# First key weights in three loads, first x turned in four parts, and a new written order for one gated attention kernel

## The chip, the cores and the metric

The kernel runs on one core of one Trainium2 chip. A time is the device time of one execution in microseconds (us). Before the change three runs gave 263.52, 263.54 and 266.09 us, with a median of 263.54 us. The engines are named as in the profile: PE is the matrix engine (PEld is its weight load), DVE, ACT and POOL are the vector, scalar and general engines, and SP only issues DMAs.

## What is computed

The input is x (2048 rows, 512 columns, bf16). Two branches are computed from it and mixed, row by row, by a gate:

```
g = sigmoid(sum(x * gate_w))                 one number per row
q, k, v = x @ wq, x @ wk, x @ wv             32 heads of 16, cut into 4 segments of 512 rows
for each segment s:
    a_dot = softmax(q k^T / 4 + causal mask) v             inside the segment
    a_mem = phi(q) M / (phi(q) z + 1e-6)                   memory of the segments before
    o     = sigmoid(beta) * a_mem + (1 - sigmoid(beta)) * a_dot
    M, z  = M + phi(k)^T v, z + sum(phi(k))                phi(t) = t+1 if t>0 else exp(t)
a = concat(o) @ wo
b = (gelu(x @ w_gate) * (x @ w_up)) @ w_down               inner width 1792
out = g * a + (1 - g) * b
```

`beta` has one value per head.

## The kernel before

**Tiling.** The work is cut into four segments (the first digit in a name: `K2_3` belongs to segment 2). A segment has x transposed in SBUF (`xT`, 512 by 512), and these groups of work, each of which holds one PSUM bank while PE fills it and until another engine has emptied it:

- `K`, `Q` (four groups each, four matmuls of 512 columns), `V` (eight half groups of four matmuls of 256 columns), `G` and `U` (14 each, the gate and up projections) and their evictions `Kev`, `Qev`, `Vev`, `Gev`, `gd` (gelu while evicting) and `h` (multiply by the up projection);
- the scores: 18 fills `st` a segment, which write all four banks of `psX`, one exponential `exp` on ACT for each (128 by 2048), and the causal mask on POOL (`msk`). `kpada` and `kpadb` on DVE spread k for the fills;
- `pv` (scores times v), whose result is turned and normalised on DVE (`tp`, `pvp`, `ota`), the memory read (`nd`, `ndp`, `otr`, `otm`) and write (`ktr`, `mz`, `mza`, `mzq`), and the outputs (`out` with `wev`, `wo` with `oev`, and the store `dma`).

There are four single PSUM banks for all groups other than `st`; the digit behind a colon in the order is the bank (`G0_5:3`), a letter is the engine of an eviction (`:a` ACT, `:d` DVE).

**What sets the order.** The order of all work is written out by hand in the string `ORDER` (some thousand words). The program walks through it, appends each task's instructions to the queue of its engine, and puts a semaphore wait before an instruction where data or a buffer is not free. Each engine then takes its own queue strictly in that order; an instruction that waits holds up all behind it on its engine. The waits on semaphores of DMAs are the same kind of wait. SP's DMA issues are a queue like the others.

**The start.** Two row blocks of the first x (`x0_0`, `x0_1`) are loaded and turned by PE against an identity matrix (`xtr0`, L786), the result is copied from `psX` to `xT` (`xev0`, L795); the other two row blocks come by transposing DMAs (`x0_t2`, `x0_t3`, L361). Until x has arrived PE multiplies constants (`warm1`, `warm2`, L383; 45 and 7 matmuls of 80 columns). The first K (L477) is computed in three kinds of pieces: `a` (input blocks 2 and 3, the first 256 rows), `b` (blocks 0 and 1, the same rows) and `c` (all four blocks, the last 256 rows, for which `x0_t2` and `x0_t3` must have landed). wk is loaded in two halves: blocks 2, 3 from SP and 0, 1 from ACT (L341).

**Other lines that matter here.** `ld_xt` (L345) loads x of a later segment in four transposing DMAs; those of segment 1 wait for `wv` to have landed. `ld_beta` loads beta to 128 partitions (8 KB in all), `betab` (L764, DVE, four copies) sorts it by head and waits for that load; `bexp` and `gqa`, `gqb`, `gfull` make the mixing factors from it. `vsh` (L518) moves 64 partitions of `vnat` by DMA as soon as the `Vev` of its four half groups are done. An order of loads within SP can hold a wait that is in the load's own list (`["wo"]`, `["wu0"]`) only if that other load stands earlier in `ORDER`.

Of the kernel before, what the change touches and what calls it, by code (L numbers as in the profile page):

```python
# [248 lines left out]
def _build(es, nc, A_x, A_wq, A_wk, A_wv, A_wo, A_beta, B_w_gate, B_w_up, B_w_down, gate_w, out):  # L249
# [132 lines left out]
    for name, n, cols in (("warm1", 45, 80), ("warm2", 7, 80)):  # L382
        one(name, PE, 3.0, [I(lambda e, cols=cols: e.matmul(BK[s0.i][:, 0:cols], ones, ones[:, 0:cols], start=True, stop=True),  # L383
                              [], [bk(s0)]) for _ in range(n)], bias=9000.0, opens=name == "warm1")
# [400 lines left out]
    for p in (1, 0):  # L785
        one(f"xtr0_{p}", PE, 4 * T_TR, [I(lambda e, q=q, kb=kb, p=p: e.transpose(  # L786
            XB[:, 1024 * p + (kb % 2) * 256 + q * 128:1024 * p + (kb % 2) * 256 + q * 128 + 128],
            pt[stage[0]][:, q, kb * 128:(kb + 1) * 128], ident[:, :]),
            [("xs", 0, 0), ("xs", 0, 1), ("pt", stage[0]), ("ident",)], [("X", p)]) for kb in (2 * p, 2 * p + 1) for q in (0, 1)])
        dst = xT[0][:, 2 * p:2 * p + 2, 0:256]  # L790
        xin = XB[:, 1024 * p:1024 * p + 512].rearrange("p (k c) -> p k c", c=256)
        wr = [("xT", 0, kb, "h0") for kb in (2 * p, 2 * p + 1)]
        task(f"xev0_{p}", [
            (ACT, 0.477, [I(lambda e, dst=dst, xin=xin: e.activation(dst, xin, ACTF.Copy), [("X", p)], wr)]),
            (DVE, 0.335, [I(lambda e, dst=dst, xin=xin: e.tensor_copy(dst, xin), [("X", p)], wr)])], L_DVE)  # L795
# [79 lines left out]
U0_13:3 U0_10:2 h0_10 Q2_1:1 Qev2_1:d exp0_2C st0_2D mz0:0 U0_7:2 U0_9:1 pvp0_10 h0_13 exp0_2D phqb1_0 st0_2E exp0_2E phka1_0 h0_7 mza0 h0_9 ota0_0
phqa1_2 kpadb1_0 G1_4:3 U0_1:2 h0_1 Gev1_4:a V1_1b:0 st0_3A G1_0:1 U0_5:3 Q2_2:2 exp0_3A Vev1_1b:a Gev1_0:a Qev2_2:a kpadb1_1 st0_3B exp0_3B U0_11:0
U0_4:1 U0_12:2 st0_3C phkb1_0 exp0_3C phqc1_0 kpada1_2 h0_4 h0_5 U0_6:1 U0_2:3 h0_11 h0_12 phqb1_2 h0_2 G1_3:0 Gev1_3:d h0_6 kpadb1_2 st0_3D phka1_2
U0_3:2 h0_3 U0_8:3 h0_8 Q2_3:0 Qev2_3:d exp0_3D phkb1_2 msk0_2A msk0_2B msk0_2C msk0_3A msk0_2E msk0_2D msk0_3C goc0 msk0_3B st1_0A msk0_3D pv0_3:1230
exp1_0A st1_0B exp1_0B tp0_d20 tp0_d21 pvp0_20 tp0_d30 ota0_1 pvp0_21 tp0_d31 kpada1_3 out0_1_0:1 out0_1_1 out0_1_2 V2_0a:2 Vev2_0a:d G1_9:3 V2_1b:0
Vev2_1b:d wev0_1:d st1_0C G1_8:2 G1_10:0 G1_11:1 gelu1 gd1_9 G1_7:3 gd1_8 gd1_10 gd1_7 gd1_11 G1_13:2 gd1_13 G1_12:0 gd1_12 phqc1_2 phkc1_0 mzq0  # L880
pvp0_31 pvp0_30 ota0_3 V2_0b:3 Vev2_0b:d ota0_2 V2_1a:1 Vev2_1a:d out0_0_0:2 out0_0_1 out0_0_2 nd1_0:0 ndp1_0 phkc1_2 exp1_0C st1_0D exp1_0D K2_0:3
K2_2:1 wev0_0:d Kev2_0:d Kev2_2:a K2_1:0 st1_0E Kev2_1:d U1_2:2 h1_2 wo0_1:1 nd1_3:3 nd1_1:0 exp1_0E st1_1A ld_x3_2 vsh1_00 vsh2_01 ktr1_1 ktr1_0
oev0_1 ndp1_1 wo0_0:2 oev0_0 kpada2_0 vsh1_21 out0_2_0:1 nd1_2:0 msk1_0C msk1_0A exp1_1A st1_1B exp1_1B msk1_0B gz1 msk1_0E msk1_1A msk1_0D msk1_1B
out0_2_1 wo0_2:2 ndp1_2 st1_1C exp1_1C nd1_5:0 out0_2_2 ndp1_3 wev0_2:a ndp1_5 out0_3_0:3 st1_1D nd1_4:0 out0_3_1 out0_3_2 ktr1_2 dma0 vsh1_01 otr1_3
ndp1_4 otr1_0 oev0_2 phka2_0 msk1_1C wev0_3:d ktr1_3 dma1 vsh2_00 otr1_1 ld_x3_1 ld_x3_0 ld_x3_3 exp1_1D st1_2A exp1_2A gr1 msk1_1D pv1_1:1023 st1_2B
exp1_2B tp1_d01 tp1_d00 kpadb1_3 V2_2b:0 Vev2_2b:d K2_3:1 Kev2_3:a G2_3:0 pvp1_00 Gev2_3:d tp1_d10 st1_2C U1_8:1 G2_1:0 otr1_2 V2_3a:2 h1_8 Gev2_1:d
Vev2_3a:d kpadb2_0 kpadb2_1 exp1_2C st1_2D phkb2_0 exp1_2D G2_6:1 wo0_3:0 U1_3:2 pvp1_01 tp1_d11 Gev2_6:a h1_3 phka2_2 oev0_3 st1_2E U1_0:3 V2_3b:1
G2_0:2 Gev2_0:d h1_0 Vev2_3b:d exp1_2E phkb2_2 st1_3A mz1:0 G2_4:2 G2_5:3 pvp1_10 mza1 Gev2_5:d exp1_3A st1_3B exp1_3B Gev2_4:d U1_11:1 G2_2:0
Gev2_2:d ota1_0 U1_13:3 h1_13 U1_10:2 h1_10 h1_11 G2_11:0 G2_10:3 pvp1_11 phkc2_0 phkc2_2 ota1_1 otm1_0 otm1_1 G2_12:2 G2_9:1 st1_3C gelu2 gd2_11
gd2_12 G2_7:0 G2_13:2 gd2_10 gd2_9 gd2_7 gd2_13 G2_8:3 gd2_8 U1_7:1 U2_9:0 K3_0:2 h1_7 U2_5:3 Q3_0:1 phqa2_0 h2_9 h2_5 Qev3_0:d Kev3_0:d exp1_3C  # L890
st1_3D exp1_3D U1_1:0 U2_12:3 msk1_3A msk1_2A msk1_3B U2_13:1 h2_12 h1_1 h2_13 kpada2_1 st2_0A U1_9:2 V2_2a:3 U2_7:0 msk1_2D msk1_2B msk1_2E h1_9
Vev2_2a:d vsh2_20 dma2 dma3 ktr2_0 ktr2_2 vsh2_21 exp2_0A phqb2_0 msk1_3D msk1_2C msk1_3C st2_0B h2_7 kpada2_2 pv1_3:1230 tp1_d21 exp2_0B tp1_d20
V3_1a:2 Vev3_1a:a st2_0C exp2_0C pvp1_21 tp1_d31 U1_6:1 Q3_1:2 V3_0a:0 st2_0D h1_6 pvp1_20 Vev3_0a:d Qev3_1:a V3_2b:1 U1_4:2 U1_5:0 exp2_0D st2_0E
exp2_0E tp1_d30 phqc2_0 h1_5 h1_4 ota1_2 Vev3_2b:a U1_12:3 h1_12 pvp1_31 pvp1_30 out1_1_0:0 st2_1A V3_1b:2 out1_1_1 V3_3a:3 exp2_1A st2_1B msk2_0B
msk2_0D Vev3_3a:a exp2_1B out1_1_2 U2_4:1 msk2_0E goa1 gob1 kpadb2_3 kpada2_3 msk2_0C msk2_0A msk2_1A ota1_3 h2_4 otm1_2 otm1_3 K3_1:3 mzq1 Vev3_1b:a
wev1_1:a st2_1C msk2_1B goc1 U2_1:2 Q3_3:1 V3_0b:0 Kev3_1:d kpada3_0 h2_1 Qev3_3:d kpadb2_2 exp2_1C msk2_1C st2_1D V3_2a:3 U2_6:2 exp2_1D Vev3_2a:a
wo1_1:1 Vev3_0b:d kpadb3_0 h2_6 oev1_1 st2_2A msk2_1D pv2_1:0231 exp2_2A st2_2B exp2_2B tp2_d00 pvp2_00 phqa2_2 tp2_d01 tp2_d10 pvp2_10 pvp2_01
tp2_d11 out1_0_0:0 out1_0_1 st2_2C phqb2_2 out1_0_2 V3_3b:2 Vev3_3b:d wev1_0:d out1_3_0:3 phqc2_2 pvp2_11 exp2_2C st2_2D exp2_2D wo1_0:1 out1_3_1
# [46 lines left out]
```

## Time and profile before

| What | Value |
|---|---|
| Median of three runs | 263.54 us |
| The profiled execution's own time | 263.46 us |
| Its span, first to last instruction | 261.7 us |
| Around the span (263.46 - 261.7) | 1.8 us |
| PE busy | 257.5 us, 98% of the span |
| ACT, DVE, POOL busy | 203.2, 198.0 and 98.4 us |
| 72 exponentials (L609) | 1877 ns each |
| Moved by DMA | 16.50 MB |

The span runs from the first to the last instruction of the core. The busy time of PE contains modelled ends of matmuls, so that a busy PE is not yet PE at its peak pace; the chain of waits and the times at which matmuls begin tell more. A row of the timeline is: start, duration, engine, line, operation, out<-in, count, and in brackets the idle time before it and what ended that. For a DMA the duration is that of its issue; the list of DMA issues gives the time from the start of an issue to the last byte's landing.

### The profile page before, as it was taken

What the parts mean: (1) busy time and instruction counts of PE and PEld (TensorE: products, weight loads), DVE (VectorE), ACT (ScalarE), POOL (GpSimd) and SP (SyncE); (2) the same over time, 40 slices, a digit from 0 to 9 for tenths busy, and PEclk for the clock granted to TensorE, in tenths of its full rate; (3) what the DMA queues carried; (4) which work ended last, traced back from release to release, by engine and by line L of the source; (5) the groups of instructions that cost most, each with busy time, mean ns of one, the idle gap of its engine ahead of it and who ended that gap; (6) DMA issues with size and microseconds to landing.
All of it is one profiled execution on the core that took longest, in us unless ns stands there. A gap on an engine that the chain in (4) does not pass through costs nothing.

```text
span 261.7 us, 6706 instructions
## 1 busy us (share of the span) xinstructions
PE 257.5 (98%) x2849; PEld 122.1 (47%) x2849; DVE 198.0 (76%) x412; ACT 203.2 (78%) x171; POOL 98.4 (38%) x163
## 2 busy tenths in 40 slices
...
DMA packets 31990, 16.50 MB, mean 63 GB/s; under 512 B 21592, under 2 KB 31960, under 8 KB 31960
## 3 DMA queue, kind: packets, MB, share of 16 engines
...
q10 hardware_dynamic: 688, 0.85, 1.0%
...
q14 instruction: 8, 0.07, 0.1%
...
## 4 chain that ended last, share of the span: by engine, by line
PE 98%; DVE 0%; issue 0%; DVEq 0%
PE psD L449 48%; PE psD L735 19%; PE psX L602 9%; PE psD L644 6%; PE psD L499 6%; PE psD L749 5%; PE psD L477 1%; PE psD L547 1%; PE psD L383 1%; PE psD L577 1%; DVE xT L795 0%; DVE ost L753 0%; PE psX L786 0%; DVEq L818 0%; PE psD L769 0%
## 5 line engine op out<-in xcount | busy, mean ns | idle before, releaser
L609 ACT ACTIVATE pt<-psX 128x2048 bf16<-128x2048 f32 x72 | 135.1, 1877 | 28.3 <-PE psX L602 26.8
L615 POOL TENSOR_TENSOR pt<-pt,ctri 128x256 bf16<-128x256 bf16 x128 | 91.8, 727 | 129.2 <-ACT pt L609 124.7
L449 PE MATMUL psD<-xT,wu 128*128 128x512 bf16 x224 | 54.6, 380 | 0.0
L449 PE MATMUL psD<-xT,wg 128*128 128x512 bf16 x224 | 53.4, 379 | 0.0
L735 PE MATMUL psD<-wd,gb 128*128 128x512 bf16 x224 | 53.2, 380 | 0.0
L720 DVE TENSOR_TENSOR gb<-psD,gb 128x512 bf16<-128x512 f32 x56 | 37.2, 681 | 10.8 <-PE psD L449 10.7
L449 PEld LDWEIGHTS psD<-xT,wg 128*128 128x128 bf16 x224 | 20.8, 98 | 24.7 <-issue 1.3
L735 PEld LDWEIGHTS psD<-wd,gb 128*128 128x128 bf16 x224 | 20.7, 98 | 24.3 <-issue 2.1
L449 PEld LDWEIGHTS psD<-xT,wu 128*128 128x128 bf16 x224 | 20.2, 98 | 24.7 <-issue 2.6
L602 PE MATMUL psX<-qT,kD 32*128 32x192 bf16 (+7 forms) x512 | 28.6, 287 | 0.0
L530 DVE STREAM_TRANSPOSE tT<-psD 128x512 f32<-128x512 f32 x32 | 21.8, 701 | 5.4 <-PE psD L644 4.9
L443 DVE CAST gb<-psD 128x512 bf16<-128x512 f32 x20 | 13.6, 688 | 13.0 <-PE psD L449 13.0
L602 PEld LDWEIGHTS psX<-qT,kD 32*128 32x128 bf16 x512 | 8.2, 92 | 25.1 <-ACT pt L609 13.6
L499 PE MATMUL psD<-wv,xT 128*128 128x257 bf16 (+1 forms) x128 | 18.2, 273 | 0.0
L753 DVE SCALAR_TENSOR_TENSOR ost<-psD,gtok,wds 128x512 bf16<-128x512 f32 (+1 forms) x17 | 11.9, 711 | 7.7 <-PE psD L749 7.6
L668 DVE SCALAR_TENSOR_TENSOR ob<-tT,gq,rc 128x256 bf16<-128x256 f32 x32 | 16.7, 522 | 1.1
L703 ACT ACTIVATE gb<-psD 128x512 bf16<-128x512 f32 x28 | 15.0, 594 | 3.3 <-PE psD L449 3.2
L644 PE MATMUL psD<-pt,vsh 64*17 64x192 bf16 (+7 forms) x512 | 17.1, 283 | 0.0
L644 PE MATMUL psD<-pt,vnat 64*17 64x192 bf16 (+7 forms) x512 | 17.1, 283 | 0.0
L449 PE MATMUL psD<-xT,wq 128*128 128x512 bf16 x64 | 16.3, 379 | 0.0
L749 PE MATMUL psD<-wo,oT 128*128 128x512 bf16 (+1 forms) x68 | 16.1, 367 | 0.0
L499 PEld LDWEIGHTS psD<-wv,xT 128*128 128x128 bf16 x128 | 11.8, 97 | 6.6 <-issue 1.3
...
## 6 DMA issues: line engine op xcount, KB each, us to landing
out_dram<-ost SPq DMA_DIRECT2D x15, 128.0 KB, 1.9
...
wq<-in_A_wq_dram SPq DMA_DIRECT2D x2, 256.0 KB, 3.5
wv<-in_A_wv_dram SPq DMA_DIRECT2D x1, 512.0 KB, 4.3
wo<-in_A_wo_dram SPq DMA_DIRECT2D x1, 512.0 KB, 4.5
```

Source lines behind the costliest of these rows:

```text
L449: one(name, PE, n * T_MM, [I(lambda e, i=i: e.matmul(BK[sl.i][:, :], lhs(i), rhs(i), start=(i == 0), stop=(i == n - 1)), reads(i), [bk(sl) ...
L499: one(f"V{s}_{m}{'ab'[hf]}", PE, 2 * T_MM, [I(lambda e, i=i, sl=sl, a=a, z=z, xs=xs: e.matmul(BK[sl.i][:, 0:z - a], xs(i), wv[:, i, a:z], ...
L530: one(f"tp{name}", DVE, 0.605, [I(lambda e, sl=sl, ti=ti: e.transpose(tT[ti][:, :], BK[sl.i][:, :]), [bk(sl)], [("tT", ti)])], bias=bias)
L602: ins.append(I(lambda e, t=t, kb=kb, ncol=ncol, c0=c0, g=g: e.matmul(XALL[:, g * 512 + c0:g * 512 + c0 + ncol], kD[(4 * s + t) % R_KD][32 ...
L609: one(f"exp{s}_{name}", ACT, 2048 * 0.000833 + 0.05, [I(lambda e: e.activation(pt[slot][:, :, :], xin, ACTF.Exp, scale=ATT_SCALE), [("X",) ...
L615: ins.append(I(lambda e, mv=mv: e.tensor_tensor(mv, mv, cm, ALU.mult), [("pt", slot), ("causal",)], [("pt", slot)]))
L644: ins.append(I(lambda e, kb=kb, slot=slot, c0=c0, n=n, g=g, r0=r0, sl=banks[j], va=va: e.matmul(BK[sl.i][32 * g:32 * g + 17, 64 * kb:512], ...
L668: I(lambda e, ti=ti, ri=ri, t=t, j=j, dst=dst: e.scalar_tensor_tensor(out=dst, in0=t_rows(ti), scalar=gq[:, 2 * t + j:2 * t + j + 1], in1= ...
L703: t = one(f"gd{s}_{ft}", ACT, 0.485, [I(lambda e, gi=gi, f=f, sl=sl: e.activation(gb[gi][:, f, :], BK[sl.i][:, :], ACTF.Gelu_apprx_tanh), ...
L720: one(f"h{s}_{ft}", DVE, 0.605, [I(lambda e, sl=sl, gi=gi, f=f: e.tensor_tensor(gb[gi][:, f, :], BK[sl.i][:, :], gb[gi][:, f, :], ALU.mult ...
L735: mm.append(I(lambda e, fb=fb, gi=gi, f=f, q=q, sl=sl: e.matmul(BK[sl.i][:, :], gb[gi][:, f, q], wd[:, fb, :], start=(fb == 0), stop=(fb = ...
L749: one(f"wo{s}_{qt}{sfx}", PE, 4 * T_MM * w / 512, [I(lambda e, kb=kb, q=q, so=so, c=c, w=w: e.matmul(BK[so.i][:, 0:w], oT[:, kb, q], wo[:, ...
```

## The change

The change has three parts. wk is loaded in three pieces: block 2 from SP, block 3 from ACT, and blocks 0 and 1 behind it from ACT. The transposes of the first x are four tasks of two transposes each instead of two of four, each with its own bank of `psX`, and each is copied out by itself (128 by 256), two of the copies on ACT and two on DVE. The two runs of constant matmuls become one, of 52 matmuls of 66 columns. And `ORDER` is another one: the tasks are the same otherwise, but their order, 34 of the evictions' engines, and the banks are different.

```
-    for eng, h in ((SP, 1), (ACT, 0)):
-        ld_w(f"wk{h}", eng, wk[:, halves[h], :], wsrc(A_wk)[:, halves[h], :], [("wk", 2 * h), ("wk", 2 * h + 1)], 0.25)
+    for eng, nm, c in ((SP, "2", slice(2, 3)), (ACT, "3", slice(3, 4)), (ACT, "0", slice(0, 2))):
+        ld_w(f"wk{nm}", eng, wk[:, c, :], wsrc(A_wk)[:, c, :], [("wk", i) for i in range(c.start, c.stop)], 0.125)
...
-    for name, n, cols in (("warm1", 45, 80), ("warm2", 7, 80)):
-        one(name, PE, 3.0, [I(lambda e, cols=cols: e.matmul(BK[s0.i][:, 0:cols], ones, ones[:, 0:cols], start=True, stop=True),
-                              [], [bk(s0)]) for _ in range(n)], bias=9000.0, opens=name == "warm1")
+    one("warm1", PE, 3.0, [I(lambda e: e.matmul(BK[s0.i][:, 0:66], ones, ones[:, 0:66], start=True, stop=True),
+                             [], [bk(s0)]) for _ in range(52)], bias=9000.0, opens=True)
...
-    for p in (1, 0):
-        one(f"xtr0_{p}", PE, 4 * T_TR, [I(lambda e, q=q, kb=kb, p=p: e.transpose(
-            XB[:, 1024 * p + (kb % 2) * 256 + q * 128:1024 * p + (kb % 2) * 256 + q * 128 + 128],
+    for kb in (2, 3, 0, 1):
+        one(f"xtr0_{kb}", PE, 2 * T_TR, [I(lambda e, q=q, kb=kb: e.transpose(
+            XB[:, 1024 * kb + q * 128:1024 * kb + q * 128 + 128],
...
+        dst, xin, wr = xT[0][:, kb, 0:256], XB[:, 1024 * kb:1024 * kb + 256], [("xT", 0, kb, "h0")]
+        task(f"xev0_{kb}", [
+            (ACT, 0.38, [I(lambda e, dst=dst, xin=xin: e.activation(dst, xin, ACTF.Copy), [("X", kb)], wr)]),
+            (DVE, 0.25, [I(lambda e, dst=dst, xin=xin: e.tensor_copy(dst, xin), [("X", kb)], wr)])], L_DVE)
```

The beginning of `ORDER`, before and after:

```
-ld_x0_0 ld_wk1 ld_x0_1 warm1:0 ident xtr0_1 xev0_1:d xtr0_0 warm2 xev0_0:d vones0 masks ld_wk0 causal1 gwz ld_x0_t2 ld_x0_t3 ld_wq0 ld_wq1 ld_gw
-causal0 consts K0_1a:1 K0_3a:2 K0_3b K0_2a:3 K0_0a:0 K0_2b K0_0b K0_1b K0_0c K0_2c K0_3c K0_1c Kev0_0:d Kev0_2:d kpadb0_0 kpadb0_2 causal kpada0_0
-Kev0_3:a Q0_0:0 ld_wg0b Qev0_0:a Q0_1:3 st0_0A gwtr:2 Kev0_1:d gwev Q0_3:0 ld_wv ld_wg0 Qev0_1:d V0_1b:1 V0_3a:2 V0_3b:3 exp0_0A Qev0_3:d Vev0_3a:a
-Vev0_1b:a st0_0B Vev0_3b:d kpada0_2 kpada0_1 V0_0b:0 V0_1a:2 V0_2a:1 Vev0_0b:d G0_6:3 Gev0_6:d Vev0_1a:d Vev0_2a:d exp0_0B st0_0C exp0_0C Q0_2:0
-G0_2:3 V0_2b:2 ld_x1_2 ld_x1_1 ld_x1_3 ld_x1_0 ld_beta st0_0D Vev0_2b:a exp0_0D Gev0_2:d kpadb0_1 Qev0_2:d phka0_0 V1_2b:1 V0_0a:3 G1_6:2 V1_0b:0
...
-st0_1D phkc0_0 betab Kev1_1:d kpada1_1 G0_4:1 G0_3:0 Gev0_4:d Kev1_0:d Gev0_3:d Kev1_3:a ld_wd0 ld_wu0 ktr0_1 ktr0_0 vsh1_20 ld_wo V1_1a:2 Vev1_1a:d
+ident causal1 ld_x0_1 ld_wk3 ld_wk0 vones0 ld_x0_0 ld_wk2 ld_x0_t2 ld_x0_t3 warm1:0 xtr0_2 xtr0_3 xtr0_0 xtr0_1 ld_wq0
+xev0_3:a ld_wq1 ld_wv masks xev0_1:a gwz xev0_2:d K0_3a:1 K0_1a:2 K0_0a:3 xev0_0:d K0_3b K0_1b K0_0b K0_3c K0_1c
+Kev0_1:d Kev0_3:a kpadb0_3 K0_0c kpadb0_1 Kev0_0:d kpada0_0 K0_2a:0 K0_2b Q0_0:1 kpadb0_0 ld_gw ld_wg0b Q0_1:2
+Qev0_1:d phka0_0 K0_2c ld_wd0 ld_wg0 Qev0_0:a st0_0A exp0_0A Kev0_2:d kpada0_2 Q0_2:3 Q0_3:1 gwtr:2 gwev Qev0_3:a
+ld_wg1 ld_x1_2 V0_0a:0 Vev0_0a:a st0_0B V0_2b:2 V0_2a:1 Vev0_2b:d Vev0_2a:d exp0_0B V0_0b:0 V0_1a:2 V0_1b:1 Vev0_1a:d
+Vev0_1b:d Vev0_0b:a st0_0C ld_x1_0 V0_3a:0 V0_3b:2 Vev0_3a:d Vev0_3b:d ld_x1_1 G0_2:1 G0_6:0 ld_x1_3 vsh0_01 vsh0_21
+ld_beta Qev0_2:a ld_wu1 ld_x2_0 ld_wd1 ld_x2_2 Gev0_2:d exp0_0C phkb0_0 Gev0_6:d st0_0D phkc0_0 kpada0_1 ktr0_0
+exp0_0D G0_5:3 G1_6:2 Gev1_6:a betab V1_2b:1 Gev0_5:d st0_0E V1_3a:0 Q1_2:2 G0_1:3 exp0_0E st0_1A exp0_1A consts
+causal0 causal msk0_0E gz0 gr0 bexp gqa msk0_0C msk0_0B gfull Vev1_2b:d Qev1_2:d Q1_0:1 G1_5:2 Gev1_5:a Vev1_3a:d
...
```

The end of `ORDER`, before and after:

```
-out3_3_2 wo3_2:3 oev3_1 wev3_2:a oev3_2 wo3_3b:1 dma13 dma14 wev3_3:a oev3_3b dma15b wo3_3a:2 oev3_3a dma15a
+wev3_2:d wo3_2:1 oev3_2 wo3_3b:2 dma13 wo3_3a:0 dma14 wev3_3:a oev3_3b dma15b oev3_3a dma15a
```

More of the change, by code (lines that the diff above doesn't have):

```diff
@@ L784, in _build @@
     XB = XALL.bitcast(BF)
-    for p in (1, 0):
-        one(f"xtr0_{p}", PE, 4 * T_TR, [I(lambda e, q=q, kb=kb, p=p: e.transpose(
-            XB[:, 1024 * p + (kb % 2) * 256 + q * 128:1024 * p + (kb % 2) * 256 + q * 128 + 128],
+    for kb in (2, 3, 0, 1):
+        one(f"xtr0_{kb}", PE, 2 * T_TR, [I(lambda e, q=q, kb=kb: e.transpose(
+            XB[:, 1024 * kb + q * 128:1024 * kb + q * 128 + 128],
             pt[stage[0]][:, q, kb * 128:(kb + 1) * 128], ident[:, :]),
[L789 to L795, printed above, removed]
+            [("xs", 0, 0), ("xs", 0, 1), ("pt", stage[0]), ("ident",)], [("X", kb)]) for q in (0, 1)])
+        dst, xin, wr = xT[0][:, kb, 0:256], XB[:, 1024 * kb:1024 * kb + 256], [("xT", 0, kb, "h0")]
+        task(f"xev0_{kb}", [
+            (ACT, 0.38, [I(lambda e, dst=dst, xin=xin: e.activation(dst, xin, ACTF.Copy), [("X", kb)], wr)]),
+            (DVE, 0.25, [I(lambda e, dst=dst, xin=xin: e.tensor_copy(dst, xin), [("X", kb)], wr)])], L_DVE)
     head_gates()
@@ L867 @@
-G0_2:3 V0_2b:2 ld_x1_2 ld_x1_1 ld_x1_3 ld_x1_0 ld_beta st0_0D Vev0_2b:a exp0_0D Gev0_2:d kpadb0_1 Qev0_2:d phka0_0 V1_2b:1 V0_0a:3 G1_6:2 V1_0b:0
-Vev1_2b:d phka0_2 st0_0E Vev0_0a:d Vev1_0b:d G0_1:1 Gev1_6:a exp0_0E Gev0_1:d Q1_2:3 V1_3b:2 V1_3a:0 kpada0_3 Qev1_2:d Vev1_3a:d phkb0_2 phkc0_2
-Vev1_3b:d st0_1A gz0 exp0_1A gr0 Q1_0:1 V1_0a:3 G1_5:0 Vev1_0a:d Gev1_5:d st0_1B Q1_1:2 K1_0:3 exp0_1B phkb0_0 ld_wu1 ld_x2_0 G0_5:0 Qev1_0:d kpadb0_3
-vsh0_21 st0_1C exp0_1C Qev1_1:d ld_x2_1 ld_x2_3 ktr0_3 ld_wg1 Gev0_5:d V1_2a:1 K1_3:2 K1_1:0 vsh0_01 Vev1_2a:a vsh0_20 ld_x2_2 ktr0_2 vsh0_00 ld_wd1
@@ L875 @@
[L875 to L898, printed above, removed]
```

77 lines of the change are left out of this document (58 added, 19 removed).

## The prediction

> **What bounds the kernel now.** I read the page's busy shares and its chain first, then the busy time by stage, then the chain in order of time.
>
> ```profile
> span 261.7 us, 6706 instructions
> ...
> PE 257.5 (98%) x2849; PEld 122.1 (47%) x2849; DVE 198.0 (76%) x412; ACT 203.2 (78%) x171; POOL 98.4 (38%) x163
> ...
> PE 98%; DVE 0%; issue 0%; DVEq 0%
> ```
>
> ```profile
> 5.30:258.70 253.40, 253.39 (x2789) 118.14 (x2789) 196.49 (x409) 201.96 (x170) 94.75 (x142) 1.00 0.27 60
> ```
>
> ```profile
> 0.82 3.16 PE psD L383 x45
> ...
> 5.21 0.10 issue
> 5.31 3.65 PE psD L477 x32
> 8.96 1.73 PE psD L449 x8
> ...
> 15.08 0.97 PE psD L449 x4
> 16.05 0.33 PE psX L602 x8
> 16.38 1.83 PE psD L449 x8
> 18.22 0.44 PE psD L499 x4
> ```
>
> The columns of the second block are window, length, then busy time of PE, PEld, DVE, ACT and POOL. From the first K matmul to the last output matmul PE has no gap (253.39 of 253.40). The chain's pieces show that this is real pace, not a stretched end: a group of four 512-column matmuls takes 0.86 (1.73 for two), a V half 0.44, a fill 0.33, and a group in front of a fill 0.97, so entering a fill costs about 0.1. Nothing but PE's own work sets the time between 5.3 and 258.7.
>
> This decides how the change must be priced. The new order holds the same groups, 72 fills that again stand apart from each other, and the short pieces of the memory work (`nd`, `mz`) in slightly different company. Counted with these durations its PE work from first K to last wo is the 253.3 of before, within 0.1. So **the body can't gain**. It can only lose, wherever the new order lets PE wait. Gains can come from the 5.3 us ahead of K and the 3 us behind the last matmul.
>
> **The head.**
>
> ```profile
> 1.25 0.41 SPq L341 DMA_DIRECT2D wk<-in_A_wk_dram  x1
> 1.71 2.59 SPq L361 DMA_TRANSPOSE xT<-in_A_x_dram  x2
> 4.35 1.09 SPq L341 DMA_DIRECT2D wq<-in_A_wq_dram  x2
> ```
>
> ```profile
> 4.49 0.43 PE L383 MATMUL psD<-const-bfloat16-1.0 128*128 128x80 bf16 x7
> ...
> 10.62 0.39 PE L602 MATMUL psX<-qT,kD 32*128 32x512 bf16 x4
> ```
>
> ```profile
> wq<-in_A_wq_dram SPq DMA_DIRECT2D x2, 256.0 KB, 3.5
> ...
> wk<-in_A_wk_dram ACTq DMA_DIRECT2D x1, 256.0 KB, 4.2
> wk<-in_A_wk_dram SPq DMA_DIRECT2D x1, 256.0 KB, 3.9
> ...
> pt<-in_A_x_dram SPq DMA_DIRECT2D x1, 128.0 KB, 2.5
> ```
>
> ```profile
> DMA to landing us min/median/max: 3.4/3.8/4.2
> ```
>
> ```profile
> L507 ACT ACTIVATE vnat<-psD 128x256 bf16<-128x256 f32 x10 | 3.7, 383 | 0.9 <-PE psD L499 0.9
> ...
> L795 DVE COPY xT<-psX 128x512 bf16<-128x512 bf16 x2 | 0.8, 420 | 4.4 <-PE psX L786 4.4
> ```
>
> The first K waits for wk as much as for the copy that the chain names: SP's half is issued at 1.25 and lands 3.9 later, at 5.15, and the second copy ends at 5.21. In the change the first pieces hold 128 KB: between the 2.5 of an x block and the 3.9 of a whole half, so landing at 3.75 to 5.15. The constants: 45 matmuls of 80 columns took 3.16, the later 7 took 0.43. With about 0.2 for the drain of the last one that is 66 ns each at first and 33 later, and 256 columns of K took 114 (3.65 over 32). The 52 of 66 columns take 54 ns each if columns set the pace and 66 if instructions do, 2.8 to 3.4 in all; as the instructions went at 33 later, columns do, and the transposes start at 3.68 instead of 3.78. ACT copies blocks 3 and 1 at 383 each by the nearest row (256 columns), DVE blocks 2 and 0 at 210 to 420; block 3 is there at about 4.75 and the first K can begin near 4.9, 0.4 earlier.
>
> Little of it is kept. All K pieces and two Q groups still stand ahead of the first fill, and K's `c` pieces need `x0_t3`. The row of landings is that of the two turned x blocks: the first landed 4.2 after its issue at 1.71, the second 3.4 after 3.05, at 6.44. wq's second half is issued at 4.97 and lands at 8.5. Neither issue moves, and the bytes ahead of them are the same. From 6.55 follow three `c` (3 x 0.44), `K0_2a` and `K0_2b` (0.44), two Q (1.73) and `K0_2c` (0.53 with the entry): the first fill begins at 10.55. By wq (third matmul of Q0_0 at 8.6) it is 10.43. Before it began at 10.62. So the gain is 0.07 to 0.19, up to 0.45 if both land earlier, and a loss of 0.15 if the constants go at 66 ns. **I take -0.15** and count on from a first fill at 10.45.
>
> Here the Trainium skill speaks against the change: "TensorE: Matmul & The Clock Gate", Part 1, says that PE runs at half clock until a window of about 3.4 us was busy, and Part 4 that transposes don't count as busy. The rows agree on the two paces; the switch came between 3.98, where the constants end, and 4.49, so it came while transposes ran, and whether they count no row shows.
>
> **The loads behind it, and beta.** Here the order moves most. SP now issues wd0, wg0 and wg1 ahead of the four x loads of segment 1, then two `vsh`, then beta. And DVE has `betab`, which waits for beta, directly ahead of `Gev0_5`, which empties bank 3 for `G0_1:3`.
>
> ```profile
> 10.82 5.54 SPq L345 DMA_TRANSPOSE xT<-in_A_x_dram  x4
> 16.41 0.58 SPq L341 DMA_DIRECT2D omem<-in_A_beta_dram  x1
> ...
> 24.80 0.71 SPq L518 DMA_DIRECT2D vsh<-vnat  x1
> 25.55 2.57 SPq L345 DMA_TRANSPOSE xT<-in_A_x_dram  x2
> ...
> 34.71 1.23 SPq L341 DMA_DIRECT2D wd<-in_B_w_down_dram  x2
> 35.99 0.58 SPq L341 DMA_DIRECT2D wu<-in_B_w_up_dram  x1
> 36.61 5.52 SPq L573 DMA_TRANSPOSE phkt<-phk  x2
> ```
>
> ```profile
> wo<-in_A_wo_dram SPq DMA_DIRECT2D x1, 512.0 KB, 4.5
> ...
> out_dram<-ost SPq DMA_DIRECT2D x2, 64.0 KB, 1.6
> ...
> omem<-in_A_beta_dram SPq DMA_DIRECT2D x1, 8.0 KB, 4.8
> ```
>
> ```profile
> 13.37 0.43 DVE L506 CAST vnat<-psD 128x256 bf16<-128x256 f32 x1 [0.62 <-PE psD L499]
> ```
>
> ```profile
> L443 DVE CAST gb<-psD 128x512 bf16<-128x512 f32 x20 | 13.6, 688 | 13.0 <-PE psD L449 13.0
> ...
> L764 DVE COPY betab<-omem 32x8 bf16<-32x8 bf16 x4 | 0.6, 159 | 0.1
> ```
>
> Beta takes 4.8 from issue to landing though it is 8 KB. Before, `betab` stood far behind its landing: DVE idled 0.1 ahead of it. The chain after, counted from the end of `V0_3b` on PE, which is 6.5 behind the first fill's start (three fills 1.0, two Q 1.7, eight V halves 3.5, two entries and small ones 0.3), at 16.94:
>
> - `Vev0_3b` is done 0.54 later (0.11 turn, 0.43 copy); `vsh0_21` waits for it, issue 0.05 + 0.71; beta's issue begins 1.34 behind `V0_3b`, at 18.3;
> - landing +4.8 at 23.1; `betab` +0.65 (four copies and a turn), `Gev0_5` +0.69, PE's turn 0.1: `G0_1` at 24.5;
> - PE arrives there 6.06 behind `V0_3b`, at 23.0: `G0_2` 0.86, `G0_6` 0.97, fill 0.33, `G0_5` and `G1_6` 1.73, `V1_2b` 0.53, fill 0.33, `V1_3a` 0.45, `Q1_2` 0.86.
>
> PE stalls 1.5, if SP has its four x loads issued by then. They start at 10.82 (behind wv) and need 5.1 to 5.5 when free: 16.4 at the latest, ahead of `vsh0_21`. But 2.7 MB of weights are now queued ahead of them. The nearest case is the pair at 36.61, issued right behind 2.7 MB: 5.52 where a free pair takes 2.57.
>
> ```profile
> 37.00:40.00 3.00, 3.00 (x111) 1.57 (x117) 2.15 (x5) 2.09 (x3) 1.90 (x3) 1.00 1.01 349
> 40.00:43.00 3.00, 3.00 (x63) 1.34 (x43) 2.96 (x7) 2.97 (x3) 1.40 (x2) 1.00 1.11 366
> ```
>
> The last column is GB/s. At 349 to 366 the weights behind wv (10.8, less what it shares) run until about 17.5. If the x loads are held until then, the two `vsh` and beta follow to 19.4, and the stall is 2.6. I take the middle, x issued by 17.2, beta at 18.55, and **a stall of 1.8** (bounds: none if beta lands in the 1.6 of the 64 KB store, 2.6 if all is held). x itself would land about 20 to 21, where `G1_6` wants its last block at 20.6: a stall of at most 0.5, inside the same 1.8, as the later of two waits on one path counts. Behind `Gev0_5` wait `causal`, which POOL's masks need (pv is 15 us away), and three evictions, each due over 0.5 later than it comes.
>
> **The rest.** Of the evictions 18 go from DVE to ACT and 16 the other way, between engines that are 76% and 78% busy: nothing, and up to half an eviction (0.35) where one is late. `wo` is issued behind `vsh2_01`; from the end of `V2_1a` to `wo0_1` are 6.7, the eviction and two issues take 2.1 and the load 4.5: it just fits. At the end `wev3_2` moves to DVE:
>
> ```profile
> 257.89 1.53 DVE L753 SCALAR_TENSOR_TENSOR ost<-psD,gtok,wds 128x512 bf16<-128x512 f32 x3 [1.84 <-PE psD L749]
> ```
>
> DVE had 1.84 idle there, so its 0.75 is covered; if it weren't, the three last evictions would start up to 0.75 later. The tail stays: 0.
>
> **Sum** against the profiled 263.46 (0.08 under the median of 263.54): -0.15 + 1.8 + 0 = 265.1. A stall of PE at 23 us is kept to the end, as nothing behind it has slack.
>
> **Rivals.**
>
> 1. **Not slower: beta is in time.** If it lands within 3.3 of its issue (the 1.5 of stall is then gone) and the x loads aren't held, PE never waits: 263.46 less 0.15 = 263.3 (263.0 to 263.6). For it: 64 KB land in 1.6 and 8 KB should not need more; against it: the one row of beta says 4.8, in a stretch where little else was queued. The skill's "DMA: Bandwidth & Descriptors", "Anatomy of one DMA", gives 2.0 us plus bytes over 436 GB/s (for the GpSimd path), by estimate 2.0 here, which would end the stall; the row's 4.8 disagrees. 28%.
> 2. **The queue is slower than I take.** x of segment 1 lands over 1 us later than counted, or `pv0_1` meets late `vsh0` transfers (SP issues them behind wu1, wd1 and five transposes). Stall 2.8 to 5: 266.1 to 268.3, at 266.7. For it: the pair that took 5.52. 14%.
> 3. **The clock stays at half pace for another stretch**, as PE idles about 0.4 between transposes and K with no constants to fill it. The switch came some 3.5 after the first matmul at 0.82; another 3.5 would last until 7.8, and from 4.9 on half of that is lost, 1.4, as the paces of 66 and 33 ns say. What the wait for wq covers (0.3) comes off, and where beta is held by the queue its stall shortens by the rest: 265.1 to 266.2. Against it: the old idle time ahead of K was about as long. 6%.
>
> The forecast, 264.3 to 266.0, has 50%; 2% is left for what I don't see. **Range** 262.9 to 266.5: it takes in the forecast, the not slower case, the third and the lower end of the second, some 85%. One per cent is 2.6 us, about what a measurement of this kernel tells from no change (one of the three runs lay 2.6 off): faster 0.01, same 0.83, slower 0.16. The likeliest case alone is slower by 0.3 to 0.9%.
>
> **What would show it.** Right: K's first matmul at 4.8 to 5.0 and the first fill at 10.3 to 10.6; one PE gap of 1 to 2.6 us near 23, ahead of an L449 group that waits for DVE's L443; DVE idle ahead of `betab`, ended by beta's DMA; elsewhere PE without gaps and the same 3 us behind the last matmul. Wrong: no idle time ahead of L764 (rival 1), a gap ahead of `G1_6` ended by the x loads (rival 2), K matmuls at 213 ns apart (rival 3), or gaps later in the body, which I price at nothing.

## The result, and the profile after

The changed kernel takes 266.0 us (median of 10 runs, 265.37 to 266.37), the kernel before 264.09 on the same chip (10 runs): 1.0068 times as long, with a 95% interval of 1.0051 to 1.0084. The forecast was 265.1, with 262.9 to 266.5 as its range. A time here and below is the median of all runs, and a ratio with its interval is of the fast ones, which are all but the slowest run of experiment 2. The profiled execution took 265.67, 2.2 more than the 263.46 of before.

From the page of the changed kernel, the span, the busy times and the shares of the chain:

```profile
span 263.9 us, 6669 instructions
...
PE 254.8 (97%) x2815; PEld 121.3 (46%) x2849; DVE 199.6 (76%) x414; ACT 203.9 (77%) x171; POOL 98.0 (37%) x163
...
PE 83%; DVE 6%; SPq 5%; DMA 4%; issue 2%; DVEq 0%
```

34 matmul records are missing (2815 of 2849; the weight loads are complete), so PE's busy time can't be set against the 257.5 of before. Nor does the share of the chain measure the loss. Before, PE made 98% of it and now 83%, but the later experiment 8, which loses almost nothing, has 83% too, and experiment 3 has 92%: where the chain goes round by DMAs, or meets short pieces of other engines and matmul records that are missing, PE's share falls at no cost. What tells is the one long stretch off PE, from the start to 26. The chain in order of time (start, duration, what), from 6 to 25:

```profile
6.44 4.06 DMA wv<-in_A_wv_dram
...
10.51 2.05 SPq L345
12.56 0.04 issue
12.61 2.99 SPq L345
15.60 0.04 issue
15.64 1.41 SPq L345
17.05 0.04 issue
17.10 2.10 SPq L345
...
19.31 0.71 SPq L517
20.02 0.04 issue
20.07 0.59 SPq L517
20.66 0.04 issue
20.70 2.99 DMA omem<-in_A_beta_dram
...
23.72 0.16 DVE betab L763
...
24.49 0.69 DVE gb L442
```

This is the prediction's path link by link: `wv` lands, SP issues segment 1's four x loads (L345), then two `vsh` (L517), then beta; beta lands, `betab` runs, and only then `Gev0_5` (the `gb` at 24.49) frees the bank for `G0_1`. (Line numbers are mostly one less than before.)

The timeline of PE shows the head and the end of the path; then the changed kernel's waits (total, times, longest):

```profile
4.49 3.97 PE L476 MATMUL psD<-xT,wk 128*128 128x256 bf16 x28
...
10.56 0.40 PE L601 MATMUL psX<-qT,kD 32*128 32x512 bf16 x4
...
25.24 1.04 PE L448 MATMUL psD<-xT,wg 128*128 128x512 bf16 x4 [1.35 <-DVE gb L442]
```

```profile
DVE betab L763 <- DMA omem<-in_A_beta_dram: 2.6, 1, 2.6
...
PEld psD L448 <- DMA xT<-in_A_x_dram: 1.4, 3, 0.6
```

K begins at 4.49 instead of 5.31, but the first fill at 10.56 instead of 10.62. PE then meets two waits: 0.6 for x (ahead of the last matmuls of `G1_6`, near 21) and 1.35 ahead of `G0_1` at 25.24.

### The profile page after: what moved, and what is told of

It is laid out like the page before. It is cut to its first block, busy times and chain, and to the rows that moved or that the text cites. A ratio compares the mean times of both kernels' runs of the same rounds, so it can differ in the third digit from the quotient of the medians.

```text
span 263.9 us, 6669 instructions
## 1 busy us (share of the span) xinstructions
PE 254.8 (97%) x2815; PEld 121.3 (46%) x2849; DVE 199.6 (76%) x414; ACT 203.9 (77%) x171; POOL 98.0 (37%) x163
## 4 chain that ended last, share of the span: by engine, by line
PE 83%; DVE 6%; SPq 5%; DMA 4%; issue 2%; DVEq 0%
PE psD L448 41%; PE psD L734 17%; PE psX L601 7%; PE psD L643 6%; PE psD L748 5%; PE psD L498 4%; SPq L345 3%; DMA wv<-in_A_wv_dram 2%; DMA xT<-in_A_x_dram 1%; DMA omem<-in_A_beta_dram 1%; PE psD L546 1%; DVE gb L719 1%; DVE omem L560 1%; DVE tT L529 1%; PE psD L576 1%
## 5 line engine op out<-in xcount | busy, mean ns | idle before, releaser
L448 PE MATMUL psD<-xT,wu 128*128 128x512 bf16 x216 | 53.6, 380 | 1.0 <-issue 0.5
L448 PE MATMUL psD<-xT,wg 128*128 128x512 bf16 x217 | 52.2, 380 | 2.1 <-DVE gb L442 1.3
L719 DVE TENSOR_TENSOR gb<-psD,gb 128x512 bf16<-128x512 f32 x56 | 37.9, 685 | 19.7 <-PE psD L448 19.2
L734 PE MATMUL psD<-wd,gb 128*128 128x512 bf16 x217 | 51.9, 379 | 0.9 <-issue 0.5
L448 PEld LDWEIGHTS psD<-xT,wu 128*128 128x128 bf16 x224 | 20.3, 98 | 25.0 <-issue 2.6
L498 PE MATMUL psD<-wv,xT 128*128 128x256 bf16 (+1 forms) x128 | 18.2, 273 | 0.0
L667 DVE SCALAR_TENSOR_TENSOR ob<-tT,gq,rc 128x256 bf16<-128x256 f32 x32 | 16.9, 527 | 1.1
L442 DVE CAST gb<-psD 128x512 bf16<-128x512 f32 x19 | 13.0, 685 | 3.8 <-PE psD L448 3.4
L448 PE MATMUL psD<-xT,wq 128*128 128x512 bf16 x59 | 15.2, 380 | 0.6 <-issue 0.4
L748 PE MATMUL psD<-wo,oT 128*128 128x512 bf16 (+1 forms) x64 | 15.3, 366 | 0.4 <-issue 0.2
L739 ACT ACTIVATE wds<-psD,omgt 128x512 f32<-128x512 f32 x8 | 5.5, 685 | 11.1 <-PE psD L734 11.1
## 6 DMA issues: line engine op xcount, KB each, us to landing
wg<-in_B_w_gate_dram SPq DMA_DIRECT2D x1, 896.0 KB, 10.9
```

Source lines behind the costliest of these rows:

```text
L448: one(name, PE, n * T_MM, [I(lambda e, i=i: e.matmul(BK[sl.i][:, :], lhs(i), rhs(i), start=(i == 0), stop=(i == n - 1)), reads(i), [bk(sl) ...
L498: one(f"V{s}_{m}{'ab'[hf]}", PE, 2 * T_MM, [I(lambda e, i=i, sl=sl, a=a, z=z, xs=xs: e.matmul(BK[sl.i][:, 0:z - a], xs(i), wv[:, i, a:z], ...
L667: I(lambda e, ti=ti, ri=ri, t=t, j=j, dst=dst: e.scalar_tensor_tensor(out=dst, in0=t_rows(ti), scalar=gq[:, 2 * t + j:2 * t + j + 1], in1= ...
L719: one(f"h{s}_{ft}", DVE, 0.605, [I(lambda e, sl=sl, gi=gi, f=f: e.tensor_tensor(gb[gi][:, f, :], BK[sl.i][:, :], gb[gi][:, f, :], ALU.mult ...
L734: mm.append(I(lambda e, fb=fb, gi=gi, f=f, q=q, sl=sl: e.matmul(BK[sl.i][:, :], gb[gi][:, f, q], wd[:, fb, :], start=(fb == 0), stop=(fb = ...
L748: one(f"wo{s}_{qt}{sfx}", PE, 4 * T_MM * w / 512, [I(lambda e, kb=kb, q=q, so=so, c=c, w=w: e.matmul(BK[so.i][:, 0:w], oT[:, kb, q], wo[:, ...
```

## The experiments

Each is an edit of `ORDER` alone, in the changed kernel unless it says otherwise.

**1. `betab` behind the eviction it held up.**

```
-... Gev1_6:a betab V1_2b:1 Gev0_5:d ... gr0 bexp gqa msk0_0C msk0_0B gfull Vev1_2b:d ... Gev0_1:d K1_0:3
+... Gev1_6:a V1_2b:1 Gev0_5:d ... gr0 msk0_0C msk0_0B Vev1_2b:d ... Gev0_1:d betab bexp gqa gfull K1_0:3
```

> The changed kernel with `betab` and the three small copies fed by it (`bexp`, `gqa`, `gfull`) moved behind `Gev0_1`; the loads stay as they are. Theory A (the loss comes from two DMA waits near 20 to 25 us: 0.6 at `G1_6` for x, 1.5 at `G0_1` for beta through `betab`): the second wait has nothing of PE behind it any more, the first stays, and as PE comes 0.6 late to `G0_1` anyway nothing new is late there; span 263.9 - 1.5 = 262.4, about 264.2 in time, 1.001 of before. Rival B (the new order of groups and evictions costs the time, all along the body): DVE's idle time ahead of `betab` goes but the time stays, 265.5 to 266.0, 1.006 to 1.008 of before. Theory C (the two waits are one path, as the prediction counted them, and the x wait grows when the other goes): between the two, 264.8.

Measured: 264.54, ratio 1.0014 (1.0003 to 1.0025). From 1.0068 this is 0.54%, 1.4 us, for a move of some small copies. The wait for x stays:

```profile
PEld psD L448 <- DMA xT<-in_A_x_dram: 1.2, 3, 0.5
```

So theory A holds and B falls. C's 264.8 lies at the edge of the interval (264.2 to 264.8), but the wait for x didn't grow, as C needs. (The span of 262.7 in its profile holds 0.4 of a later head: the first fill began at 10.96 there.)

**2. Beta's load ahead of the weights.**

```
-... kpadb0_0 ld_gw ld_wg0b ... vsh0_01 vsh0_21 ld_beta Qev0_2:a ...
+... kpadb0_0 ld_gw ld_beta ld_wg0b ... vsh0_01 vsh0_21 Qev0_2:a ...
```

> The changed kernel with the load of beta issued right behind the gate's weights, ahead of wd0, wg0 and wg1; `betab` stays ahead of `Gev0_5`. Theory A: beta lands before 14, DVE has no idle time ahead of `betab` that a DMA ends, the wait of 0.6 at `G1_6` for x stays (SP still has its x loads behind the same weights): span 262.4, time 264.2, 1.001 of before. Rival B (body order): unchanged, 265.5 to 266.0. By the prediction's 4.8 from issue to landing beta lands near 14, by the 3.0 of the changed kernel's row near 12.

Measured: 267.97 (six runs, 265.07 to 269.80), ratio 1.0116 (1.0078 to 1.0155): slower than before by more than the changed kernel is, against both theories, though the two intervals overlap. Beta lands at 15.8, later than expected, and `betab` no longer waits, as expected. But PE does, and longer. First its timeline, then busy times in stretches of 2 us (PE, PEld, DVE, ACT, POOL, then granted clock, DMA share and GB/s):

```profile
20.67 1.67 PE L448 MATMUL psD<-xT,wg 128*128 128x512 bf16 x6 [3.42 <-DMA wg<-in_B_w_gate_dram]
```

```profile
10.00:12.00 2.00, 2.00 (x15) 0.90 (x13) 1.83 (x5) 0.95 (x2) 0.00 (x0) 1.00 0.56 170
12.00:14.00 2.00, 2.00 (x21) 1.12 (x20) 0.48 (x2) 2.00 (x4) 0.00 (x0) 1.00 0.86 256
...
20.00:22.00 2.00, 1.33 (x6) 0.72 (x8) 0.48 (x1) 0.00 (x0) 0.00 (x0) 0.95 0.44 47
22.00:24.00 2.00, 2.00 (x12) 0.42 (x11) 1.41 (x3) 0.64 (x1) 0.00 (x0) 0.50 1.00 200
24.00:26.00 2.00, 2.00 (x8) 0.82 (x7) 1.87 (x7) 1.24 (x1) 0.00 (x0) 0.70 0.78 92
```

Two things happen. First, the weights come later: wg0 lands at 20.3 instead of 16.9, and `G0_2` waits 3.42 for it. The edit does more than the expectation says, as `ld_beta` has a wait of its own, for wq's second half, which `ld_wd0` hasn't. Standing ahead of wd0, it holds wd0 up as well. SP's issues:

```profile
8.37 0.38 SPq L341 DMA_DIRECT2D omem<-in_A_beta_dram  x1
8.79 0.43 SPq L341 DMA_DIRECT2D wd<-in_B_w_down_dram  x1
```

In the changed kernel wd0 is issued at 7.34. wg0 follows at 9.26 instead of 8.11, so that 1.15 of its 3.4 are the later issue. The other 2.3 lie in its way from issue to landing, 11.1 in place of 8.8; why it takes longer isn't shown. Between 10 and 14 the DMA engines move 170 and 256 GB/s, where the changed kernel moves 342 and 380 (below). Second, behind that idle time PE is granted half its clock for about 3 us. `G0_2` is 3.37 later than the same group in experiment 3 (17.30 there), `G0_1` 4.97 later (28.11 against 23.14), though PE stands still nowhere between: the slow clock costs 1.6. The Trainium skill's "TensorE: Matmul & The Clock Gate", Part 1, has the rule that an idle window of about 3.4 us brings PE back to half clock; this run agrees, and the 1.35 of the changed kernel, behind which the clock stays at 1.00, does too. It doesn't happen in every run of this edit: three of the six have a mean granted clock of 0.993 to 0.994 and took 267.44 to 268.56, two have 0.999 and took 265.07 and 266.73, and the longest, 269.80, has 0.987.

**3. The weights issued later.**

```
-... ld_wd0 ld_wg0 ... ld_wg1 ld_x1_2 ... ld_x2_0 ld_wd1 ld_x2_2 ... ld_wu0 ktr0_1 Q2_1:1 ...
+... ld_wg0 ... ld_x1_2 ... ld_x2_0 ld_wg1 ld_x2_2 ... ld_wu0 ktr0_1 ld_wd1 ld_wd0 Q2_1:1 ...
```

> The changed kernel with wg1 issued behind x2's first block and wd0 and wd1 much later, as the kernel before had it; beta and `betab` stay. Theory A (the weights ahead of segment 1's x loads hold SP's issue of them, 8.7 instead of 5.5): SP has issued the four by 16.4, x lands by 18.5, the 0.6 at `G1_6` is gone, beta is issued behind `vsh0_21` near 18.3 and lands 3.0 to 4.8 later, 21.3 to 23.1: the wait at `G0_1` is 0 to 1.5, so the time is 263.4 to 264.9, and near 263.5 if 3.0 is the landing. Rival B (body order): 265.5 to 266.0. Rival D (the x loads are slow for another reason, such as four of them in a row behind wv): SP still needs over 8 us for them, and the time stays.

Measured: 263.94, ratio 0.9990 (0.9979 to 1.0001), span 261.8. SP's issues, DVE, PE and the list of DMA issues (the last column is issue to landing):

```profile
10.75 5.06 SPq L345 DMA_TRANSPOSE xT<-in_A_x_dram  x4
```

```profile
21.35 0.74 DVE L763 COPY betab<-omem 32x8 bf16<-32x8 bf16 x4 [0.25 <-DMA omem<-in_A_beta_dram]
```

```profile
23.14 1.03 PE L448 MATMUL psD<-xT,wg 128*128 128x512 bf16 x4
```

```profile
omem<-in_A_beta_dram SPq DMA_DIRECT2D x1, 8.0 KB, 3.0
```

SP needs 5.06 for the four x loads, beta is issued at 18.37, and `betab` waits 0.25 in place of 2.6. `G0_1` begins at 23.14. The changed kernel has the same order on PE and begins it at 25.24: 2.10 later, and its span is 2.1 longer. So all of the loss lies ahead of `G0_1`, and nothing behind it adds to it.

**4. Both.** The edits of 1 and 3 together.

> The weights later as in the run before this one, and `betab` with its three copies behind `Gev0_1`. Theory A: neither wait is left, PE runs without a gap over 0.2 from K to the last matmul: span 263.9 - 2.1 = 261.8, time 263.5, 0.999 to 1.001 of before. Rival B (body order): 265.5 to 266.0, 1.006 of before or more. If it comes out at 264.2 or above with both waits gone, the order of the body has a cost of its own of 0.5 or more, which the prediction priced at nothing.

Measured: 263.78, ratio 0.9980 (0.9969 to 0.9992). With both waits gone the new order costs nothing against before; this is the only version here whose interval lies below 1, by 0.2%. The profiled spans, 261.9 and 261.7, don't show that gain.

**5. The head alone**: the changed program, with the order of the kernel before but for its head.

```
-ld_x0_0 ld_wk1 ld_x0_1 warm1:0 ident xtr0_1 xev0_1:d xtr0_0 warm2 xev0_0:d vones0 masks ld_wk0 causal1 ...
+ld_x0_0 ld_wk2 ld_x0_1 warm1:0 ident xtr0_2 xtr0_3 xtr0_0 xtr0_1 xev0_3:a xev0_1:a xev0_2:d xev0_0:d vones0 masks ld_wk3 ld_wk0 causal1 ...
```

> The order of the kernel before with the head of the change alone: wk in three loads, x's first blocks turned in four transposes and copied by both engines, one run of constants. Theory A (the first fill hangs on x's third and fourth block and on wq, whose loads are issued no earlier): K begins near 4.5 instead of 5.3 and the first fill within 0.15 of before; span 261.6 +- 0.15, ratio 0.999 to 1.000. Rival (K is the bound of the head): the 0.8 are kept, span 260.9, ratio 0.997.

Measured: 269.32, ratio 1.0200 (1.0167 to 1.0233). This says nothing of the head, as the edit has a fault: `ld_wk3` and `ld_wk0` are issues on ACT, and they stand behind ACT's two copies. They were issued at 4.74 and 5.11.

```profile
8.16 0.80 PE L476 MATMUL psD<-xT,wk 128*128 128x256 bf16 x3 [3.26 <-DMA wk<-in_A_wk_dram]
10.20 4.78 PE L476 MATMUL psD<-xT,wk 128*128 128x256 bf16 x28 [1.24 <-DMA wk<-in_A_wk_dram]
```

```profile
10.20 3.48 PE psD L476 x16
```

It shows the price of issues behind a copy: 3.26 and 1.24 of waiting, and behind them 16 matmuls at 217 ns each where the kernel before takes 114. That is half pace, but not a fall to it: the transposes ahead of the wait are 107 ns apart, as at half pace, so PE hadn't reached full pace yet. The row of the granted clock says 1.00 here; the matmuls' spacing shows the pace.

**6. The weights alone**, in the kernel before.

```
-... Q0_3:0 ld_wv ld_wg0 Qev0_1:d ... ktr0_3 ld_wg1 Gev0_5:d ... Kev1_3:a ld_wd0 ld_wu0 ...
+... Q0_3:0 ld_wv ld_wd0 ld_wg0 ld_wg1 Qev0_1:d ... ktr0_3 Gev0_5:d ... Kev1_3:a ld_wu0 ...
```

> The kernel before with one part of the change alone: wd0 behind wv and wg1 behind wg0, so that 2.7 MB of weights are queued ahead of the four x loads of segment 1; beta and `betab` stay where before has them. Theory A (SP can't hand out the transposing loads while the weights fill the queue): SP needs over 8 us for the four instead of 5.5, x lands from 20 on where `V1_2b` wants it at 18.9; PE waits 2 to 2.6 there, nothing waits for `betab`; span 261.7 + 2.3 = 264.0, ratio 1.009. Rival (it was the new order of SP's other work): SP needs 5.5 and the time stays, ratio 1.000. If PE stands idle for over 3 us at one place, the granted clock falls behind it, as in the run with beta ahead of the weights, and it costs 1.5 more: 1.014.

Measured: 266.55, ratio 1.0093 (1.0061 to 1.0125). SP's issues and PE:

```profile
10.71 8.48 SPq L345 DMA_TRANSPOSE xT<-in_A_x_dram  x4
```

```profile
16.20 0.38 PE L449 MATMUL psD<-xT,wg 128*128 128x512 bf16 x1 [0.81 <-DMA wg<-in_B_w_gate_dram]
17.58 0.60 PE L449 MATMUL psD<-xT,wg 128*128 128x512 bf16 x2 [1.01 <-DMA wg<-in_B_w_gate_dram]
...
21.35 1.05 PE L499 MATMUL psD<-wv,xT 128*128 128x257 bf16 x8 [0.23 <-DMA xT<-in_A_x_dram]
```

The size is about the expected one and SP is held as expected. Three of the six runs have a granted clock of 1.00 and took 265.66 to 266.18, the profiled one among them; the other three have 0.994 and took 266.92 to 267.72, so the median mixes two cases. The expectation had a second case for a fallen clock, at 1.014; why only some runs have it no profile shows. The place is another: most of the wait (1.82) is for wg behind wd0, and only 0.23 for x. So wd0 ahead of wg has a price of its own, which the changed kernel escapes only because its first G groups come later.

**8 and 7. One weight at a time**: wd0 alone behind `ktr0_1` (experiment 8), then wg1 alone behind `ld_x2_0` (experiment 7).

```
-... K0_2c ld_wd0 ld_wg0 ... ld_wu0 ktr0_1 Q2_1:1 ...
+... K0_2c ld_wg0 ... ld_wu0 ktr0_1 ld_wd0 Q2_1:1 ...
```

```
-... Qev0_3:a ld_wg1 ld_x1_2 ... ld_x2_0 ld_wd1 ...
+... Qev0_3:a ld_x1_2 ... ld_x2_0 ld_wg1 ld_wd1 ...
```

> The changed kernel with wd0 alone moved back (issued behind `ktr0_1`), wg1 stays ahead of segment 1's x loads. Theory A, sizes: 1.8 MB instead of 2.7 are ahead of x, the last of it lands 2.4 earlier than the 19.4 of the changed kernel, at 17.0; SP has its x loads out by about 17, x lands by 19 (in time for `G1_6` at 20), beta is issued behind `vsh0_21` at 18.5, lands near 21.5, no wait above 0.3; span 262.0, ratio 1.000. Rival (any weight load of that size ahead is enough to hold SP to the end): waits of 0.3 to 1 stay, span 262.7, ratio 1.003.

> The changed kernel with wg1 alone moved behind x2's first block; wd0 stays ahead. It is the counterpart of the run with wd0 alone moved (SP's four x loads took 6.58, x landed by 19.19, no wait). Theory A (what counts is the bytes ahead of x, 1.8 MB in both): SP needs 6 to 7 for them, x lands by 19.3, beta is issued near 18.6 and lands near 21.7, no wait above 0.1, span 262.0, ratio 1.000. Rival E (wd0's place counts, as it delays wg0 and wg0b behind it, which `G0_2` wants at 17.2): wg0 lands at 17 or later instead of 15.1, and PE waits up to 0.5 at `G0_2`; span 262.2 to 262.6, ratio 1.001 to 1.003.

Measured: 263.98, ratio 1.0008 (0.9988 to 1.0028), span 262.0, for wd0; 263.99, ratio 0.9998 (0.9983 to 1.0014), span 262.3, for wg1. Either move is enough. With wd0 later, SP's issues:

```profile
10.57 6.58 SPq L345 DMA_TRANSPOSE xT<-in_A_x_dram  x4
```

They end at 17.15; wg1, the last weight ahead of them, lands at 17.3. With wg1 later, PE:

```profile
17.79 1.67 PE L448 MATMUL psD<-xT,wg 128*128 128x512 bf16 x7 [0.51 <-DVE vnat L505]
```

`G0_2` is 0.5 later than in experiment 3, as wg0b behind wd0 lands at 17.5 (the label names DVE, which is long done there). That is rival E, and the 0.5 stands in the span; in the times it can't be told from the others.

**9. Beta first and the weights later**: the edits of 2 and 3 together.

> All weights later, as in the third run, and beta's load directly behind the gate's weights. It asks why the load of 8 KB ahead of the weights made them land 3 us later in the second run. Theory X (its 128 small pieces of 64 bytes hold up whatever is queued behind them): wg0 lands at 17 to 18 instead of 15.1, `G0_2` wants it at 17.2: a wait of 0 to 1, span 261.8 to 262.8, ratio 0.999 to 1.003, with the DMA rate between 10 and 14 below the 187 and 300 of the third run. Theory Y (it takes the 2.7 MB behind it, or it was chance): wg0 lands by 15.6, no wait, span 261.8, ratio 0.999.

Measured: 263.80, ratio 0.9989 (0.9972 to 1.0006), span 262.1.

wg0's issue and its time to landing:

```profile
9.46 0.43 SPq L341 DMA_DIRECT2D wg<-in_B_w_gate_dram  x1
...
wg<-in_B_w_gate_dram SPq DMA_DIRECT2D x1, 448.0 KB, 7.0
```

wg0 lands at 16.45 instead of the 15.10 of experiment 3, but it is issued 1.25 later (8.21 there): wq's second half, for which it waits, came later in this run (ACT's wg0b, which beta doesn't stand ahead of, went out at 9.05 instead of 8.21), and beta's own issue takes 0.4. From issue to landing it needs 7.0 here and 6.9 in experiment 3. The rate of 82 GB/s between 10 and 12, where experiment 3 has 187, is that later start. So theory X isn't borne out here, and nobody waits; the 2.3 of experiment 2 need the other weights or were chance, and stay open.

**10. The head alone, again**, with the two issues of wk ahead of ACT's copies.

```
+ld_x0_0 ld_wk2 ld_x0_1 ld_wk3 ld_wk0 warm1:0 ident xtr0_2 xtr0_3 xtr0_0 xtr0_1 xev0_3:a xev0_1:a xev0_2:d xev0_0:d vones0 masks causal1 ...
```

> The order of the kernel before with the head of the change alone, this time with the two later pieces of wk issued on ACT's queue right behind x's second block, ahead of ACT's copies (in the run before, they stood behind the copies and were issued at 4.74 and 5.11 instead of about 1.2). Theory A (the head is held by loads that are not issued earlier: wk's last piece lands at 5.60 in the changed kernel, x's fourth block at 6.42, wq at 7.4 and 8.1): K begins at 4.5, halts for the last piece of wk, and the first fill begins 0 to 0.3 ahead of before's 10.62; span 261.4 to 261.7, ratio 0.999 to 1.000. Rival (K's start is the bound): the 0.8 are kept, span 260.9, ratio 0.997. As the order of the body is the old one, no wait for beta or x follows in either case.

Measured: 264.02, ratio 1.0005 (0.9992 to 1.0018): no gain.

```profile
4.51 1.08 PE L476 MATMUL psD<-xT,wk 128*128 128x256 bf16 x4
5.99 3.60 PE L476 MATMUL psD<-xT,wk 128*128 128x256 bf16 x28 [0.40 <-DMA wk<-in_A_wk_dram]
```

K begins 0.8 earlier and then halts for wk's last piece, which lands at 5.86 here. Its first eight matmuls go at half pace, until 6.8, and the first fill begins at 11.25, 0.63 behind the kernel before. The profiled execution was the slowest of the twelve (265.35); PE also waits 1.22 for wg at 17.25 in it. So its other stretches say little of the median.

## Why the prediction was right, and where not

**The body has no slack and can only lose: right.** With the waits taken out, the new order has a span of 261.8 and before has 261.7. The rest, priced at nothing, is nothing.

**The head, -0.15: too large.** K came earlier than the 4.9 forecast, and the first fill at 10.56 instead of 10.45. That is a gain of 0.06, and the head alone gives none that can be measured. The reason given, that x's later blocks aren't issued earlier, holds: `x0_t3` lands at 6.42, the first `c` piece begins at 6.55, and the fill at 10.56 where the prediction's own sum from 6.55 gave 10.55; the rest of the -0.15 was a choice. No wait for wq shows. wk's last piece is a second bound of this kind, which the prediction didn't name (PE waits 0.23 for it in experiment 4 and 0.40 in experiment 10).

**The x loads issued by 17.2: wrong, the step that failed.** SP was done at 19.20, beyond even the 17.5 given for "all held". The changed kernel's rate by stretch shows why:

```profile
10.00:12.00 2.00, 2.00 (x15) 0.93 (x14) 1.83 (x5) 1.00 (x1) 0.00 (x0) 1.00 1.05 342
12.00:14.00 2.00, 2.00 (x22) 1.15 (x21) 0.42 (x2) 2.00 (x4) 0.00 (x0) 1.00 1.05 380
14.00:16.00 2.00, 2.00 (x26) 1.53 (x23) 1.38 (x5) 2.00 (x4) 0.00 (x0) 1.00 1.05 390
16.00:18.00 2.00, 1.91 (x20) 1.18 (x14) 1.32 (x5) 2.00 (x2) 0.00 (x0) 1.00 2.01 316
18.00:20.00 2.00, 2.00 (x17) 0.65 (x15) 1.70 (x3) 1.74 (x3) 0.00 (x0) 1.00 0.82 131
```

```profile
8.52 0.56 SPq L341 DMA_DIRECT2D wg<-in_B_w_gate_dram  x1
10.51 8.68 SPq L345 DMA_TRANSPOSE xT<-in_A_x_dram  x4
```

```profile
wg<-in_B_w_gate_dram SPq DMA_DIRECT2D x1, 896.0 KB, 10.9
```

The rate taken for the weights (349 to 366) was right until 17 (382 GB/s between 16 and 17) and fell after it, to 251 and then 28 between 18 and 19, so that wg1 landed at 8.52 + 10.9 = 19.4 instead of 17.5. The trace's list of packets shows a tail: wg1's last packets start one at a time, about 0.07 us apart, until 18.7, while the first packets of the x loads, begun from 17.4 on, take up to 1.7 us. The prediction priced the bytes and not this end. And "the middle" was the wrong choice between free and held: SP's last x issue ends 0.1 to 0.2 ahead of the last weight's landing in this run and in experiments 1, 2, 6, 7 and 8. The bound of 2.6 for a stall with all held was added up wrongly besides: it counts beta's 4.8 from the end of its issue (19.4), where the row counts from the start; by the prediction's own terms it is 2.1.

**Beta's landing of 4.8: wrong, the other way.** It took 3.0, and 2.9 to 3.3 in experiments 1 and 3 to 8; 4.9 in the tenth, and 7.4 and 5.5 where it stood ahead of weights. One row was no constant. The Trainium skill's "DMA: Bandwidth & Descriptors", "Anatomy of one DMA", has a fit for DMAs that GpSimd issues, which would make it 2.0 by estimate; no run came below 2.9.

**The stall of 1.8 at `G0_1`: 2.10.** The two errors, +2.15 in beta's issue (20.70 for 18.55) and -1.8 in its landing, nearly cancel: beta landed at 23.70 where 23.35 was forecast. The near hit owes something to that; with 4.8 from 20.70 the stall would have been 3.9, with 3.0 from 18.55 nothing worth a word. The wait for x (0.6, forecast at most 0.5) does lie inside the total, as the prediction counted: without beta's wait it is all that is left (experiment 1), and with it PE only reaches `G0_1` later and waits less there.

**Sum.** -0.06 + 2.1 is 2.0, of 2.2 in span and time of the profiles and 1.9 in the medians; forecast were 1.65.

**The rivals.** "Beta is in time" fell with the x issue; with beta's 3.0 and a free queue it would have held, as experiment 3 shows. "The queue is slower" was right about the queue, but paid back by beta's landing. "The clock stays at half pace" was right about the pace for a short while and wrong about the price. K's first six matmuls, in the changed kernel and then in the one before:

```profile
4.49 1.36 PE L476 MATMUL psD<-xT,wk 128*128 128x256 bf16 x6
```

```profile
5.31 0.81 PE L477 MATMUL psD<-xT,wk 128*128 128x256 bf16 x6 [0.40 <-DVE xT L795]
```

In the changed kernel they begin 190 to 250 ns apart, up to 5.7, and 109 apart from there, as before has them from the start. This is the sign that the prediction had named for this rival (213 ns apart). It cost nothing, as the `c` pieces had to wait for `x0_t3` until 6.55 anyway.
